# A linear-attention and MLP block on one core: v is never formed, column sums go to GpSimd, and nearly all projections become 64-row matmuls

## The chip, the cores and the metric

The kernel runs on one core of a Trainium2 chip. A core has a matrix engine (TensorE, "PE" in the profile; its weight loads are shown apart as "PEld"), VectorE ("DVE"), ScalarE ("ACT"), GpSimd ("POOL") and a queue engine that starts DMAs ("SP"). In this kernel PE accumulates into eight PSUM banks, and VectorE and ScalarE empty them. The metric is device microseconds for one execution. The profile counts from the first to the last instruction and is about 1.7 us shorter than that time.

The granted clock of TensorE differs from run to run (0.96 to 1.00 as a mean), so it is given with the times.

## The reference

```python
xn = layernorm(x)                              # x: 2048 tokens x 448, bf16
q, k, v = split(xn @ wqkv)                     # 16 heads of 28
pq, pk = phi(q), phi(k)                        # phi(t) = t+1 if t>0 else exp(t), + 1e-6
kv = einsum("bhsd,bhse->bhde", pk, v)          # summed over all tokens
z  = einsum("bhsd->bhd", pk)
o  = (pq @ kv) / (pq . z + 1e-6)
s  = o @ wo
g  = silu(relu(xn @ w1 + b1)**2 @ w2 + b2)     # 1792 hidden units
return x + s * g
```

As v is linear in xn, sum over tokens of pk^T v = (sum over tokens of pk^T xn) Wv. That is the identity that the change uses.

## The kernel before

The kernel keeps all on the chip. It lists operations, and a small scheduler of its own gives each engine a fixed order and assigns the PSUM banks when the program is built; at run time each engine follows its list and waits on semaphores. The 2048 tokens are 16 tiles of 128, or 4 groups of 512. The feature dimension, 448, is three chunks of 128 rows and one of 64. The transposed input `xT` holds this last chunk twice, on partitions 0 to 63 and 64 to 127, so that the 64-row remainders of two accumulators run on the two halves of the array at once (in the trace the two matmuls of such a pair start 3 to 4 ns apart):

```python
def pe_two(a, b, n, mm, reads, first):            # two accumulators
    lo, hi, full = slice(0, 64), slice(64, 128), slice(0, 128)
    if first:
        mm(e, 0, lo, 3, True, False)              # the 64-row pair
        mm(e, 1, hi, 3, True, False)
        for w in (0, 1):
            for c in range(3):                    # six 128-row matmuls
                mm(e, w, full, c, False, c == 2)
    else:
        ...                                       # six 128-row ones, then the pair

def kv(si):                                       # k and v of a token tile
    pe_two(kb, vb, D, ...)
    phi(kb, pk[:, si, :], ...)                    # ACT exp, DVE min+add, DVE max
    add("act", ... activation(out=va[:, si, :, 0:PD], in_=ps(vb)..., func=AF.Copy))

def kvt(g):                                       # pk^T v of four token tiles
    for si in range(4 * g, 4 * g + 4):
        for c in range(4):
            e.matmul(ps(kvb)[0:KA, c*PD:(c+1)*PD], va[:, si, c, 0:KA], pk[:, si, c*PD:(c+1)*PD], ...)
```

`va` has columns of ones beside v, so z comes out of the same matmuls. After the four groups, `kv` is folded with `wo`, the denominators are formed, and a last stage multiplies by w2 and writes the output.

## Time and profile before

| kernel before | value |
|---|---|
| time, first comparison | 165.28 us median of 4 runs (165.13 to 166.94) |
| span in the profile | 163.6 us |
| projections, sums and folds | 9.6 to 103.2 us |
| last stage (w2, output) | 103.2 to 163.6 us |

The page's first part (busy us, share of the span, instructions), and its fourth (the chain of waits: shares of the span by engine, then by line):

```profile
PE 153.2 (94%) x919; PEld 74.6 (46%) x927; DVE 102.2 (62%) x240; ACT 75.2 (46%) x135; POOL 20.2 (12%) x37
...
PE 89%; DMA 4%; DVE 2%; SPq 2%; issue 1%; DVEq 0%
```

PE is busy nearly always, and the chain stays on PE. To find out what PE loses while "busy", starts have to be read, as matmuls overlap. The timeline of PE around 68 us (start, duration, engine, line, operation, shape of the weights, output):

```profile
67.50 0.38 PE L595 MATMUL pb<-xT,w 128*128 128x512 bf16 x1
67.81 0.39 PE L595 MATMUL pb<-xT,w 64*128 64x512 bf16 x2
68.04 0.38 PE L595 MATMUL pb<-xT,w 64*128 64x512 bf16 x2
68.35 0.39 PE L595 MATMUL pb<-xT,w 128*128 128x512 bf16 x1
68.58 0.38 PE L595 MATMUL pb<-xT,w 128*128 128x512 bf16 x1
```

Each row after the first starts 0.31, 0.23, 0.31 and 0.23 us after the one before it. In undisturbed stretches 512-column matmuls start every 0.216 us. A step from 128 rows to 64 or back, called a mode step below, costs about 0.095 us; a pair (x2) costs no more than one matmul. The time from one start to the next is called a slot.

### The profile page before, as it was taken

What the parts mean: (1) busy time and instruction counts of PE and PEld (TensorE: products, weight loads), DVE (VectorE), ACT (ScalarE), POOL (GpSimd) and SP (SyncE); (2) the same over time, 40 slices, a digit from 0 to 9 for tenths busy, and PEclk for the clock granted to TensorE, in tenths of its full rate; (3) what the DMA queues carried; (4) which work ended last, traced back from release to release, by engine and by line L of the source; (5) the groups of instructions that cost most, each with busy time, mean ns of one, the idle gap of its engine ahead of it and who ended that gap; (6) DMA issues with size and microseconds to landing.
All of it is one profiled execution on the core that took longest, in us unless ns stands there. A gap on an engine that the chain in (4) does not pass through costs nothing.

```text
span 163.6 us, 2398 instructions
## 1 busy us (share of the span) xinstructions
PE 153.2 (94%) x919; PEld 74.6 (46%) x927; DVE 102.2 (62%) x240; ACT 75.2 (46%) x135; POOL 20.2 (12%) x37
## 2 busy tenths in 40 slices
PE   6568899999999999999999999999999999999990
PEld 6434445444435543454544444444455555555550
DVE  0688998688894756755584757399943433443373
ACT  3133677676675675766666756821121111121110
POOL 8600000000000000000000000000004432224352
PEclk9999999999999999999999999999999999999997
DMA  4999960000000000000000000000000011100013
GB/s 144 326 402 331 379 179 0 0 4 2 0 0 0 4 0 0 0 0 4 0 0 0 0 6 0 0 0 0 4 0 28 28 56 40 48 28 28 28 39 129
DMA packets 7158, 9.15 MB, mean 56 GB/s; under 512 B 556, under 2 KB 6252, under 8 KB 7148
## 3 DMA queue, kind: packets, MB, share of 16 engines
q1 hardware_dynamic: 6588, 8.09, 15.2%
q10 hardware_dynamic: 560, 0.92, 1.6%
q8 instruction: 7, 0.11, 0.3%
q14 instruction: 3, 0.02, 0.0%
HBM read 7.17 MB, written 1.84 MB: 55 GB/s over the span
## 4 chain that ended last, share of the span: by engine, by line
PE 89%; DMA 4%; DVE 2%; SPq 2%; issue 1%; DVEq 0%
PE pb L595 28%; PE pb L716 26%; PE pb L561 13%; PE pb L581 8%; PE pb L744 7%; DMA x_tok<-in_A_x_dram 4%; PE pb L626 2%; PE pb L466 2%; SPq L378 2%; PE pb L695 1%; DVE xT L478 1%; PE pb L668 1%; PE pb L649 1%; DVE st L413 0%; DVE obuf L753 0%
## 5 line engine op out<-in xcount | busy, mean ns | idle before, releaser
L595 PE MATMUL pb<-xT,w 128*128 128x512 bf16 (+1 forms) x216 | 46.8, 381 | 0.6 <-issue 0.3
L716 PE MATMUL pb<-w,r 128*128 128x448 bf16 x224 | 44.9, 353 | 0.0
L606 ACT ACTIVATE r<-pb,b1f 128x512 bf16<-128x512 f32 x56 | 35.2, 687 | 17.9 <-PE pb L595 17.9
L758 POOL TENSOR_TENSOR obuf<-obuf,x_tok 128x448 bf16<-128x448 bf16 x14 | 14.3, 1031 | 139.1 <-DVE obuf L753 139.1
L716 PEld LDWEIGHTS pb<-w,r 128*128 128x128 bf16 x224 | 21.5, 98 | 20.9 <-issue 1.3
L614 DVE TENSOR_TENSOR r<-r 128x512 bf16<-128x512 bf16 x56 | 22.4, 420 | 11.9 <-ACT r L606 11.8
L595 PEld LDWEIGHTS pb<-xT,w 128*128 128x128 bf16 (+1 forms) x224 | 17.2, 97 | 26.4 <-issue 10.9
L733 ACT ACTIVATE gbuf<-gbuf 128x448 bf16<-128x448 bf16 x16 | 9.2, 577 | 42.0 <-DVE gbuf L725 42.0
L725 DVE TENSOR_TENSOR gbuf<-pb,b2b 128x448 bf16<-128x448 f32 x16 | 10.0, 625 | 25.1 <-PE pb L716 24.7
L561 PE MATMUL pb<-w_qkv,xT 128*128 128x448 bf16 (+1 forms) x128 | 24.1, 354 | 1.7 <-DVE xT L478 1.6
L561 PEld LDWEIGHTS pb<-w_qkv,xT 128*128 128x128 bf16 (+1 forms) x128 | 9.8, 97 | 14.9 <-issue 5.6
L581 PE MATMUL pb<-xT,w_qkv 128*112 128x512 bf16 (+1 forms) x64 | 14.3, 387 | 0.0
L744 PE MATMUL pb<-msb,pqT 112*128 112x448 bf16 x64 | 13.9, 352 | 0.0
L538 ACT ACTIVATE pk<-pb 128x448 bf16<-128x448 f32 x16 | 8.7, 546 | 10.0 <-PE pb L561 10.0
L413 DVE BATCH_NORM_STATS2 st<-x_tok 128x6 f32<-128x448 bf16 x16 | 9.3, 614 | 5.9 <-DMA x_tok<-in_A_x_dram 5.9
L753 DVE TENSOR_TENSOR obuf<-pb,gbuf 128x448 bf16<-128x448 f32 x16 | 10.0, 625 | 2.1
L550 DVE SCALAR_TENSOR_TENSOR pqT<-pb,pqT 112x512 bf16<-112x512 f32 x16 | 10.7, 686 | 0.2
L538 ACT ACTIVATE pqT<-pb 112x512 bf16<-112x512 f32 x16 | 8.8, 596 | 4.4 <-PE pb L581 4.3
L550 DVE SCALAR_TENSOR_TENSOR pk<-pb,pk 128x448 bf16<-128x448 f32 x16 | 9.9, 619 | 0.2
L703 DVE TENSOR_TENSOR pqT<-pqT,pb 112x512 bf16<-112x512 bf16 x16 | 9.9, 679 | 0.0
L581 PEld LDWEIGHTS pb<-xT,w_qkv 128*112 128x112 bf16 (+1 forms) x64 | 6.9, 129 | 6.5 <-issue 3.1
L744 PEld LDWEIGHTS pb<-msb,pqT 112*128 112x128 bf16 x64 | 6.2, 97 | 5.9
(51 smaller groups left out, 81.9 us busy)
## 6 DMA issues: line engine op xcount, KB each, us to landing
out_dram<-obuf SPq DMA_DIRECT2D x16, 112.0 KB, 1.7
w<-in_B_w_dram SPq DMA_DIRECT2D x1, 1568.0 KB, 14.6
x_tok<-in_A_x_dram SPq DMA_DIRECT2D x3, 448.0 KB, 10.0
w<-in_B_w_dram SPq DMA_DIRECT2D x1, 1344.0 KB, 9.0
w_qkv<-in_A_wqkv_dram ACTq DMA_DIRECT2D x1, 672.0 KB, 5.0
x_tok<-in_A_x_dram SPq DMA_DIRECT2D x2, 224.0 KB, 4.4
w<-in_B_w_dram SPq DMA_DIRECT2D x2, 224.0 KB, 9.5
w_o<-in_A_wo_dram SPq DMA_DIRECT2D x1, 392.0 KB, 15.5
```

Of the source, the lines that this page charges most:

```text
L538: "act", lambda e, _: e.activation(out=slot, in_=ps(buf)[0:rows, 0:n], func=AF.Exp), [buf, "actw"],
L550: lambda e, _: e.scalar_tensor_tensor(out=slot, in0=ps(buf)[0:rows, 0:n], scalar=1.0 + 1e-6, in1=slot, op0=ALU.add, op1=ALU.max),
L561: return e.matmul(ps((kb, vb)[w])[:, 0:D], xT[rows, c, si * P : (si + 1) * P], w_qkv[rows, c, col : col + D], start=start, stop=stop,)
L581: return e.matmul(ps(bufs[w])[0:PD, 0:512], w_qkv[rows, c, col : col + PD], xT[rows, c, g * 512 : (g + 1) * 512], start=start, stop=stop,)
L595: return e.matmul(ps(bufs[w])[:, 0:512], w_1[rows, c, col : col + P], xT[rows, c, g * 512 : (g + 1) * 512], start=start, stop=stop,)
L606: lambda e, _, fi=fi, slot=slot, buf=bufs[w]: e.activation(out=slot, in_=ps(buf)[:, 0:512], func=AF.Relu, bias=b1f[:, fi : fi + 1]),
L614: return e.tensor_tensor(out=slot, in0=slot, in1=slot, op=ALU.mult)
L716: last = e.matmul(ps(b)[:, 0:D], r2[:, fi, si * P : (si + 1) * P], w_2[:, fi, :], start=(fi == 0), stop=(fi == NF - 1),)
L725: "dve", lambda e, _: e.tensor_tensor(out=gs, in0=ps(b)[:, 0:D], in1=b2b[:, :], op=ALU.add),
L744: last = e.matmul(ps(b)[:, 0:D], pqT[0:PD, c, si * P : (si + 1) * P], msb[0:PD, c, 0:D], start=(c == 0), stop=(c == 3),)
L753: "dve", lambda e, _: e.tensor_tensor(out=ob, in0=ps(b)[:, 0:D], in1=gs, op=ALU.mult),
L758: return e.tensor_tensor(out=ob, in0=ob, in1=x_tok[:, si, :], op=ALU.add)
```

## The change

Its intent: take PE's work down (no v, no separate k-by-v sums), take most of the mode steps out (64-row matmuls only, but for the first four k tiles, which keep the old form), and take four of ScalarE's evictions per group away. The core of the diff, with cuts:

```diff
-def kv(si): ...                        # k and v
-def kvt(g): ...                        # pk^T v, with the ones for z
+def pe_four(a, b, c, d):               # four accumulators, 64-row matmuls only
+    # lower half: a and b in four steps each, then c and d in three; upper half: c, d, then a, b
+    for lo, hi, us in ((0, 4, (a, c)), (4, 8, (b, d)), (8, 11, (c, a)), (11, 14, (d, b))):
+        for i in range(lo, hi):
+            for h in (0, 1):
+                u, k, start, stop = steps[h][i]
+                u[2](e, half[h], k, start, stop)
+def zsum(i):                           # z: running sum of pk, on GpSimd
+    add("pool", ... e.tensor_tensor(out=o[:, :], in0=pk[:, 0, :] if i == 1 else zacc[:, :],
+                                    in1=pk[:, i, :], op=ALU.add), ...)
+def token_sum(c):                      # xn^T pk over all 16 tiles, chunk c
+    for si in range(NT):
+        if c < 3:
+            e.matmul(ps(b)[:, 0:D], xn[:, si, c*P:(c+1)*P], pk[:, si, :], ...)
+        else:                          # 64 columns: even and odd tiles side by side
+            r = slice(64 * (si % 2), 64 * (si % 2) + 64)
+            e.matmul(ps(b)[r, 0:D], xn[:, si, 384:448], pk[:, si, :], ...)
+def fold_wv(): ...                     # times Wv, head by head; z from 4 one-column matmuls
@@ the order of PE
+quads(g, "Q0 H0 Q1 H1 Q2 H2 Q3 H3 ...")      # K, Q, H: k, q, h accumulators
+token_sum(0) ... token_sum(3); quads(g, "H6 H8 H7 H9"); fold_wv(); quads(g, "H10 H12 H11 H13")
@@ the start
+ln(0, 1); ln(1, 2); ln(2, 4)           # smaller layernorm steps; tiles 1 and 3 on ScalarE
+load_k("act", w_qkv, A_wqkv, "wk", D, 2 * D)  # Wk alone first, Wv last
```

The scheduler's rule also changes: a slightly later operation may be taken first if it is more urgent. The squares of h, which nothing needs until the last stage, are so put off.

## The prediction

> **What bounds it now.** TensorE. The page's first part has PE busy 94% of 163.6 us; the chain of waits puts 89% of the span on PE. In the timeline the first K/V matmul starts at 9.6 us; projections (q, k, v, h), k-by-v sums and folds run to 103.2 us; the last stage (w2, output) is untouched. Start to start, a 512-column matmul takes 0.216 us, a 448-column one 0.189 us, and two 64-row matmuls on the two halves of the array start 3 to 4 ns apart, so a pair costs one slot.
>
> **Where PE loses time.** Every step between a 128-row and a 64-row matmul adds 0.095 us to the spacing (0.312 instead of 0.216). Between 9.5 and 103.2 us some 66 such steps cost 6.5 us. This agrees with the Trainium skill, "TensorEngine Tiling (Array Packing)", Key Properties: changing the tiling mode drains the engine. Some 2.1 us more are three stalls at the start, PE waiting for VectorE's copy of xT. Hardly anything else is idle there.
>
> **What the change does to PE (estimates from those spacings).**
> - q, k, h in 64-row pairs: four accumulators still need 14 slots, so streaming is unchanged, but of the mode steps only some 14 remain (transposes, token sums, folds), 1.3 us: saves 5.2 us. The 250 additional pairs cost 3 to 7 ns each: 1.3 us back.
> - v goes: 56 slots, 10.6 us; the old k-by-v sums too, 64 x 0.053 = 3.5 us. Added: token sums, 56 slots, 10.6 us, and the fold with Wv, 1.0 us. Saves 2.5 us.
> - Start: separate layernorms, half the first weights, no v, so q/h begins sooner; but K0 now waits for two transposed tiles, and VectorE still queues the statistics of tiles 2 and 3 ahead of the first normalisation. Saves 1 to 3 us.
>
> **What moves elsewhere.** ScalarE loses 16 evictions of 0.54 us. VectorE has the same work in a shorter stage: some 14 us of phi, layernorm and xT per group plus 6 us of squares, against 17 us of PE. It fits because the squares are ordered late, into the token sums. ScalarE needs 4 x 0.69 = 2.75 us per quad of h against 3.02 us of PE: tight; I allow 1.5 us of PE waits. GpSimd takes 15 adds of about 1.1 us, off the path; by the Trainium skill, "GPSIMD Engine Reference", section 1, it shares SBUF interfaces with VectorE, so some VectorE operations may stretch; no trace here shows that yet.
>
> **Sum.** 5.2 - 1.3 + 2.5 + 2 + 0.3 (short folds) - 1.5, about 7.5 us, nearly all on the critical path: 165.4 to 157.6 us. Range 154.5 to 161.5.
>
> **What would show it.** First w2 matmul at about 95 us instead of 103.2; 64-row pairs spaced 0.216 to 0.223 us; under 20 mode steps; PE idle under 3 us between first K and first w2 matmul; token sums in 10.6 us; the last stage as long as before.
>
> **What would make it wrong.** Pairs that overlap worse in long runs (twice the weight loads): 0.01 us per slot costs 3 us. PE waiting by several us for evictions. VectorE stretched by GpSimd. w1 landing late, as h starts earlier (before, it landed at about 14 to 16 us).
>
> Chances: faster by over 2%: 0.92; within 2%: 0.07; slower: 0.01.

## More of the kernel before

VectorE's groups, by shape (count, then busy us and mean ns of one; then idle time before them):

```profile
L614 DVE TENSOR_TENSOR r<-r 128x512 bf16<-128x512 bf16 x56 | 22.4, 420 | 11.9 <-ACT r L606 11.8
L550 DVE SCALAR_TENSOR_TENSOR pk<-pb,pk 128x448 bf16<-128x448 f32 x16 | 9.9, 619 | 0.2
L432 DVE TENSOR_SCALAR xn<-x_tok,mv,rstd 128x448 bf16<-128x448 bf16 x16 | 5.5, 390 | 0.6 <-ACT rstd L425 0.6
L543 DVE TENSOR_SCALAR pk<-pk 128x448 bf16<-128x448 bf16 x16 | 4.4, 273 | 3.3 <-ACT pk L538 3.2
L446 DVE COPY xn<-xn 128x256 bf16<-128x256 bf16 x3 | 0.7, 220 | 0.0
```

These means are what the same operations are to be held against later: squares 420 ns, normalisation (`xn<-x_tok`) 390 ns, min-and-add of phi (`pk<-pk`) 273 ns, doubling of the last chunk (`xn<-xn`) 220 ns.

## The result

In the first comparison the changed kernel took 159.14 us (median of 4 runs, 159.10 to 159.31), the one before 165.28 us. The ratio, taken as the mean time of one kernel's fast runs over that of the other's of the same rounds and so not quite the ratio of the medians, is 0.961 (95% interval 0.955 to 0.967). The result is 1.5 us above the predicted 157.6 us, within the stated range. The first w2 matmul came at about 97 us, not 95.

The same parts of the page for the changed kernel:

```profile
PE 148.4 (94%) x1131; PEld 76.5 (49%) x1131; DVE 105.9 (67%) x237; ACT 70.8 (45%) x129; POOL 35.4 (22%) x49
...
PE 86%; DVE 6%; DMA 3%; SPq 2%; ACT 1%; issue 0%; DVEq 0%
```

PE's busy time falls by 4.8 us. VectorE's rises by 3.7 us, though it has almost the same operations, and 6% of the chain lie on VectorE, where it was 2%. Between the projections' matmuls the mode steps are gone, as the timeline of PE around 22 us shows: the rows start 0.21 to 0.22 us apart, and each window holds two pairs (x4), so a pair takes the time of one matmul, with nothing added:

```profile
22.20 0.59 PE L597 MATMUL pb<-xT,w 64*128 64x512 bf16 x4
22.42 0.59 PE L597 MATMUL pb<-xT,w 64*128 64x512 bf16 x4
22.63 0.59 PE L597 MATMUL pb<-xT,w 64*128 64x512 bf16 x4
22.85 0.59 PE L597 MATMUL pb<-xT,w 64*128 64x512 bf16 x4
```

Two things were not expected. First, the chain of waits between 46 and 58 us leaves PE for 8 us:

```profile
48.23 0.99 ACT pk L542 x2
49.52 1.06 DVE pk L554 x2
50.59 1.33 DVE xn L421 x2
51.91 1.21 DVE pk L547 x2
53.13 1.06 DVE pk L554 x2
54.19 1.34 DVE xn L421 x2
55.55 1.03 DVE xn L449
56.63 1.07 PE pb L463 x16
```

The transposes of the fourth group (L463) wait for the doubling of the last chunk (L449), that waits for the normalisations (L421), and these are longer than before. PE idles; the list of waits (who, for whom: us in total, times, longest) has it as its longest wait within the projections:

```profile
PE pb L463 <- DVE xn L449: 2.2, 2, 1.9
```

VectorE's groups show which operations grew:

```profile
L612 DVE TENSOR_TENSOR r<-r 128x512 bf16<-128x512 bf16 x56 | 20.6, 433 | 7.5 <-ACT r L606 7.5
L554 DVE SCALAR_TENSOR_TENSOR pk<-pb,pk 128x448 bf16<-128x448 f32 x16 | 9.6, 619 | 0.3
L421 DVE TENSOR_SCALAR xn<-x_tok,mv,rstd 128x448 bf16<-128x448 bf16 x14 | 6.2, 492 | 0.1
L547 DVE TENSOR_SCALAR pk<-pk 128x448 bf16<-128x448 bf16 x16 | 6.8, 432 | 4.6 <-ACT pk L542 4.6
L449 DVE COPY xn<-xn 128x256 bf16<-128x256 bf16 x3 | 1.5, 489 | 0.1
```

The one that reads PSUM (L554) still takes 619 ns. The other three, which read and write SBUF alone, grew: 273 to 432 ns, 390 to 492, 220 to 489. The timelines of VectorE and GpSimd, laid beside each other, say when:

```profile
50.50 1.41 DVE L421 TENSOR_SCALAR xn<-x_tok,mv,rstd 128x448 bf16<-128x448 bf16 x2
...
50.66 2.33 POOL L575 TENSOR_TENSOR zacc<-zacc,pk 128x448 f32<-128x448 f32 x2 [12.98 <-DVE pk L554]
54.34 2.15 POOL L575 TENSOR_TENSOR zacc<-zacc,pk 128x448 f32<-128x448 f32 x2 [1.34 <-DVE pk L554]
...
55.55 1.02 DVE L449 COPY xn<-xn 128x256 bf16<-128x256 bf16 x1
```

The second normalisation of the first row starts at 50.81 us, inside the first GpSimd add, and ends at 51.91, just after that add (51.78). The copy at 55.55 us starts just after the add of 55.46 us and ends just after it (56.57 and 56.49 us). Counted over the whole trace, operations that meet an add exceed the median of their own kind by 7.5 us in all, half a microsecond per add; bn_stats (the layernorm statistics, which read and write SBUF too: 611 ns alone, 617 with an add) and the PSUM-sourced phi step (618 and 624) don't grow. This agrees with the Trainium skill, "GPSIMD Engine Reference", section 1 (Specifications): GpSimd's SBUF interfaces are shared with VectorE, and instructions of VectorE in a two-port mode or with two SBUF inputs contend. The trace doesn't tell which mode an instruction ran in.

Second, after its idle time PE ran slow. The columns of this view of 57.70 to 61.00 us are the busy time and count of each engine, then the granted clock, the DMA share and GB/s. First the run of the first comparison, then a later run of the same kernel:

```profile
57.70:61.00 3.30, 3.30 (x18) 1.47 (x20) 2.08 (x5) 0.61 (x1) 0.00 (x0) 0.53 0.00 0
```

```profile
57.70:61.00 3.30, 3.30 (x32) 1.71 (x34) 2.19 (x6) 1.36 (x3) 0.00 (x0) 1.00 0.00 0
```

At a granted clock of 0.53, PE started 18 matmuls in this stretch, at 1.00 it started 32. Pairs were 0.42 us apart instead of 0.216 in the slow stretch, and the excess sums to 1.6 us. The later run has the same wait, but no slow stretch, and took 157.6 us.

The two traces suggest why. In their clock records the changes lie 3.413 us, or a multiple of it, apart, but for the last of each: in the first run at 6.73, 57.93 and 61.34 us; in the later one at 4.52 us and not again before 154.71. Counted on from 6.73 and 4.52 us in steps of 3.413, the wait of the first run lies whole in the step from 54.51 to 57.93 us, at the end of which the clock fell; that of the later run is cut in two at 55.72 us. PE's busy time (second column) in these steps, the first run and then the later one:

```profile
54.51:57.93 3.42, 1.48 (x22) 1.11 (x22) 3.39 (x6) 2.46 (x5) 1.90 (x2) 1.00 0.00 0
52.31:55.72 3.41, 2.36 (x22) 0.97 (x18) 3.38 (x6) 2.52 (x6) 1.99 (x3) 1.00 0.00 0
55.72:59.13 3.41, 2.52 (x30) 1.72 (x32) 3.41 (x8) 1.61 (x3) 0.75 (x1) 1.00 0.00 0
```

So whether the same wait costs a slow stretch would depend on where it falls on this grid. No run was made to test it.

The last stage was left alone and shows it (the columns are as above; the first row is the last stage before the change, then the changed kernel's projections and last stage):

```profile
103.20:163.60 60.40, 56.50 (x308) 28.16 (x304) 30.50 (x51) 11.83 (x19) 14.31 (x14) 0.98 0.10 31
9.10:97.35 88.25, 85.53 (x765) 42.44 (x766) 69.59 (x169) 55.68 (x102) 15.84 (x15) 0.98 0.19 57
97.35:157.60 60.25, 56.38 (x304) 28.11 (x302) 31.98 (x55) 11.98 (x20) 14.32 (x14) 0.99 0.10 31
```

### The profile page after: what moved, and what is told of

It is laid out like the page before. It is cut to its first block, busy times and chain, and to the rows that moved or that the text cites. A ratio compares the mean times of both kernels' runs of the same rounds, so it can differ in the third digit from the quotient of the medians.

```text
span 157.6 us, 2827 instructions
## 1 busy us (share of the span) xinstructions
PE 148.4 (94%) x1131; PEld 76.5 (49%) x1131; DVE 105.9 (67%) x237; ACT 70.8 (45%) x129; POOL 35.4 (22%) x49
## 4 chain that ended last, share of the span: by engine, by line
PE 86%; DVE 6%; DMA 3%; SPq 2%; ACT 1%; issue 0%; DVEq 0%
PE pb L755 27%; PE pb L597 25%; PE pb L783 8%; PE pb L585 7%; PE pb L564 6%; PE pb L626 6%; DMA b1r<-in_B_b_dram 3%; PE pb L463 3%; DVE xn L421 2%; SPq L365 2%; DVE pk L554 1%; PE pb L632 1%; DVE pk L547 1%; PE pb L734 1%; DVE xT L473 1%; DVE xn L449 1%
## 5 line engine op out<-in xcount | busy, mean ns | idle before, releaser
L597 PE MATMUL pb<-xT,w 64*128 64x512 bf16 x392 | 48.2, 381 | 0.0
L597 PEld LDWEIGHTS pb<-xT,w 64*128 64x128 bf16 x392 | 19.0, 95 | 22.6 <-issue 1.4
L612 DVE TENSOR_TENSOR r<-r 128x512 bf16<-128x512 bf16 x56 | 20.6, 433 | 7.5 <-ACT r L606 7.5
L575 POOL TENSOR_TENSOR zacc<-zacc,pk 128x448 f32<-128x448 f32 x13 | 13.7, 1055 | 46.8 <-DVE pk L554 45.4
L585 PE MATMUL pb<-xT,w_qkv 64*112 64x512 bf16 x112 | 15.7, 395 | 0.0
L564 PE MATMUL pb<-w_qkv,xT 64*128 64x448 bf16 (+1 forms) x100 | 12.8, 350 | 1.3 <-DVE xT L473 0.8
L554 DVE SCALAR_TENSOR_TENSOR pqT<-pb,pqT 112x512 bf16<-112x512 f32 x16 | 10.9, 688 | 0.3
L585 PEld LDWEIGHTS pb<-xT,w_qkv 64*112 64x112 bf16 x112 | 7.5, 133 | 5.9 <-issue 1.3
L542 ACT ACTIVATE pk<-pb 128x448 bf16<-128x448 f32 x16 | 7.8, 540 | 5.1 <-PE pb L564 5.1
L547 DVE TENSOR_SCALAR pk<-pk 128x448 bf16<-128x448 bf16 x16 | 6.8, 432 | 4.6 <-ACT pk L542 4.6
L554 DVE SCALAR_TENSOR_TENSOR pk<-pb,pk 128x448 bf16<-128x448 f32 x16 | 9.6, 619 | 0.3
```

Source lines behind the costliest of these rows:

```text
L542: "act", lambda e, _: e.activation(out=slot, in_=ps(buf)[0:rows, 0:n], func=AF.Exp), [buf, "actw"],
L554: lambda e, _: e.scalar_tensor_tensor(out=slot, in0=ps(buf)[0:rows, 0:n], scalar=1.0 + 1e-6, in1=slot, op0=ALU.add, op1=ALU.max),
L564: return e.matmul(ps(b)[:, 0:D], xT[rows, c, si * P : (si + 1) * P], w_qkv[rows, c, D : 2 * D], start=start, stop=stop)
L575: lambda e, _: e.tensor_tensor(out=o[:, :], in0=pk[:, 0, :] if i == 1 else zacc[:, :], in1=pk[:, i, :], op=ALU.add),
L585: return e.matmul(ps(b)[0:PD, 0:512], w_qkv[rows, c, m * PD : (m + 1) * PD], xT[rows, c, g * 512 : (g + 1) * 512], start=start, stop=stop,)
L597: return e.matmul(ps(b)[:, 0:512], w_1[rows, c, fi * P : (fi + 1) * P], xT[rows, c, g * 512 : (g + 1) * 512], start=start, stop=stop,)
```

## The experiments

Two theories stood for the wait at 54 us. Theory A: the GpSimd adds hold up VectorE's SBUF-to-SBUF operations; where these lie ahead of the transposes, PE waits, and then pays again with the clock. Theory B: VectorE simply has too much to do, or in a bad order, in a stage that became shorter. A third question was what the 64-row form itself is worth. Twelve runs of four executions each were made, in three jobs, each job on one chip together with the kernel before, whose medians there were 167.8, 166.4 and 166.8 us (slow runs included). The changed kernel itself ran in the second job only; the first job, on another chip, has e3 in its place, which is the same program but for 36 added matmuls.

### e1: the adds almost taken away

```diff
-o = zb if i == NT - 1 else zacc
-... out=o[:, :], in0=... zacc[:, :], in1=pk[:, i, :]
+o, w = zb if i == NT - 1 else zacc, slice(0, D if i in (1, NT - 1) else 1)
+... out=o[:, w], in0=... zacc[:, w], in1=pk[:, i, w]
```

> 13 of the 15 GpSimd adds handle one column instead of 448 (z is wrong on purpose); every engine's order is the same as in the changed kernel. Theory A (the adds hold up VectorE's SBUF-to-SBUF operations, so the transposes of group 3 wait, so PE idles 2.1 us and then runs 1.6 us longer at half clock): VectorE's tensor_scalar on pk and xn return from means of 432 and 492 ns to about 275 and 390 ns, the copy of the tails from 1023 to 220 ns, the PE wait at 54 us and the dip of the granted clock vanish, 155.4 us (154.9 to 156.2). Theory B (VectorE's work is just too much or too late for the shortened stage): the wait stays above 1 us and the time above 157.5 us.

The time was 155.49 us (155.24 to 155.62). The result is wrong, as meant. The order of every engine is the same. PE's wait at 54 us and the slow clock are gone, and VectorE's groups are as they were before the change:

```profile
L421 DVE TENSOR_SCALAR xn<-x_tok,mv,rstd 128x448 bf16<-128x448 bf16 x14 | 4.8, 391 | 0.1
L547 DVE TENSOR_SCALAR pk<-pk 128x448 bf16<-128x448 bf16 x16 | 4.4, 280 | 5.8 <-ACT pk L542 5.8
L449 DVE COPY xn<-xn 128x256 bf16<-128x256 bf16 x3 | 0.7, 223 | 0.1
```

That is theory A's number, and 2.3 us under e3 of the same job, which has the wait but in three of four runs no slow clock. B falls as the only cause: the same order and the same VectorE work cause no wait once the adds don't run beside it.

### e2: the normalisation moved out of the way, the adds left

ScalarE's `rstd` of the last four tiles was ready for computing at 45 us but stood in ScalarE's list at 50.2 us. A bonus in the scheduler moves it ahead; the list of PE and GpSimd stays the same.

```diff
 add("act", ... activation(out=rstd[:, c], in_=vep[:, c], func=AF.Exp, scale=-0.5), ...)
+.boost = 20.0 if lo == 12 else 0.0        # subtracted from the operation's latest start
```

> Correct kernel. ScalarE computes the rstd of tiles 12 to 15 right after the logarithm, 5 us earlier than in the changed kernel; VectorE can then normalise these tiles at about 45 us, before the GpSimd adds of the group start at 50.7 us. Adds, PE order and all else as in the changed kernel. Theory A as refined (contention costs only where a blocked operation lies on PE's path): the sum of VectorE's stretch stays at 5 us or more, but the PE wait at 54 us and the clock dip vanish: 155.4 us (154.9 to 156.3). Rival (any stretch of VectorE is paid for in time): 158 us or more.

The time was 155.98 us (155.81 to 156.35), and the result is correct. VectorE normalised the four tiles in one row, before the first add of that group at 50.32 us:

```profile
44.91 1.31 DVE L422 TENSOR_SCALAR xn<-x_tok,mv,rstd 128x448 bf16<-128x448 bf16 x4 [0.65 <-ACT rstd L414]
```

The wait of the transposes vanished. A small new one (0.4 us by the list of waits) stood at 56 us: an accumulator of q waited for a min-and-add that an add had stretched to 1.12 us. So order was a second ingredient: with a better order the same contention is almost free here. The 2.1 us took both, adds running beside the normalisations and normalisations standing late in the list; taking away either one removed them.

### e3: PE kept busy through the wait

```diff
+if g == 2:
+    warm(36, dur=0.01)                    # 36 matmuls on the identity, result unused
 pe_transpose([4 * g + 4, 4 * g + 5])
```

> Correct kernel. 36 matmuls on the identity (about 2.0 us) are put in front of the group-3 transposes, where PE waits; all other orders are the same. If the half-speed stretch after the wait is the clock gate answering PE's idleness, it vanishes while the wait of the transposes stays (they start at 56.6 us as before): about 157.5 us (157.2 to 158.0), and PEclk shows no dip. Rival (the dip has another cause, say power or the run of 64-row matmuls): dip stays, 159.1 us.

The median was 157.79 us; the runs were 157.40, 157.75 and 157.84 us at a granted clock of 1.00, and 159.13 us at 0.985, which is the run that was profiled. In this profile the stretch after the wait ran at full clock:

```profile
57.70:61.00 3.30, 3.30 (x45) 2.38 (x44) 3.30 (x9) 1.16 (x2) 0.30 (x1) 1.00 0.00 0
```

and the slow stretch it does have lies elsewhere, at 9.2 to 12.6 us, right at the start. This agrees with a dip that answers PE's idleness and can be prevented without shortening the wait, but it does not prove it. On the 3.413 us grid of this trace a border (56.99 us) cuts the wait (56.13 to 58.15 us) in two, so that perhaps no dip would have come without the added matmuls either; and of the four runs of the unedited kernel in after_again, below, two kept their clock too. The Trainium skill, "TensorE: Matmul & The Clock Gate", Part 1, tells of such a gate, which falls to half clock after an idle window of about 3.4 us; the window is free-running. The 3.413 us grid of the traces agrees with such a window, but it need not be wholly idle: in the trace of the first comparison about 2 us of idle time within one such stretch sufficed. Only two of the eight runs of the changed kernel have a trace, one with the dip and one without; six of the eight have the time and mean clock of one dip, but where the untraced ones had it is not known (e3's run of 159.13 us had it at the start).

### e5 and its repetition: z on PE

```diff
-zsum(i) on GpSimd, 15 adds
+for si in range(NT):                      # four column strips of 32 at once
+    r = slice(32 * (si % 4), 32 * (si % 4) + 32)
+    e.matmul(ps(b)[r, 0:D], ones[:, :], pk[:, si, :], start=(si < 4), stop=(si >= NT - 4))
+... one ScalarE eviction; the fold multiplies by 1/32 instead of 1
```

> Correct kernel. The column sums move from GpSimd to PE: 16 matmuls with a 32-column stationary of ones, on four column strips at once, and one ScalarE eviction. VectorE is free of GpSimd in the projections; PE gets about 4 slots of 0.19 us and two mode steps, 0.95 us. Theory A: 155.4 + 0.95 = 156.3 us (155.8 to 157.0), no wait at 54 us. Theory B: no gain, 159.5 to 160 us.

156.47 us (156.25 to 156.61), correct. It costs PE about 1 us more than e1, as estimated from the slots, and there is no stretch on VectorE. The repetition in the third job:

> The kernel of run e5 (column sums on PE), unedited, so that the next one stands beside it on one chip: 156.5 us again (156.2 to 156.7).

Its median was 156.60 us, from 156.01, 156.43 and 156.77 us, and one run of 158.10 us at a granted clock of 0.989. That run has no trace; this kernel has no wait at 54 us, so some clock can be lost without it.

### after_again: the changed kernel once more

> The changed kernel itself, unedited, so that it stands beside the kernel before and the next three on one chip. The first comparison gave 159.1 against 165.3 us; on the chip of the last four runs the kernel before took 166.7 to 168.9 us. If that chip or day is slower for both, the changed kernel is slower by the same 1.5%; if only the kernel before varies (its granted clock was 0.964 to 0.99 in those runs), the changed kernel stays near 159.1 us.

The four runs were 157.60 and 157.89 us at a granted clock of 0.996 and 0.998, and 159.13 and 159.50 us at 0.985 and 0.986: the same program, with a mean clock as with and without one slow stretch. Neither alternative of the expectation is quite right; both kernels vary. The kernel before took 165.0 to 165.3 us at 0.995 to 1.00, 166.4 to 166.5 us at 0.984 to 0.985, and, in its slow run, 167.7 us at 0.979 in this job. At full clock the comparison is thus about 165.1 against 157.7 us. Where the kernel before loses its clock in those runs was not seen: the runs without a profile have no trace.

### e4 and e10: q, k and h multiplied as before

```diff
-pe_four(*us)
+pe_two(us[0], us[2], False)
+pe_two(us[1], us[3], True)
```

> Correct kernel. The changed kernel with q, k and h multiplied as before: per two accumulators six 128-row matmuls and one 64-row pair (42 groups); v still not formed, the sums still on GpSimd. By the prediction the 64-row form is worth some 42 mode steps of 0.095 us, 4.0 us, minus what the additional pairs cost (0 to 1.7 us), so this run takes 162 to 163.5 us if nothing else moves. If the pairs saved less than thought: 160 us or less. The wait at 54 us may shift, as the scheduler sees another timing; its size is to be read off and taken out.

158.95 us (158.71 to 159.09), far under the 162 expected. The trace shows why: in this kernel's list the last normalisations stand at 44 to 46 us, ahead of the adds, and PE doesn't wait at 54 us nor lose its clock. Undoing the 64-row form had undone the wait too, so the comparison was blurred. e10 does it again in the kernel that has no adds:

> Run e5 with q, k and h as in run e4 (six 128-row matmuls and one 64-row pair per two accumulators). No GpSimd adds and so, in either form, no wait in the projections: the difference from e5_again is the worth of the 64-row form alone. Counting mode steps in the traces of e4 (some 44, 4.2 us) and e1 (14, 1.3 us) gives 2.9 us: 159.4 us (159.0 to 160.0). If the 64-row form were worth only what e4 against the changed kernel suggests (0 to 0.4 us), this is under 157.2 us; if as much as predicted (5.2 less 1.3 us), 160.4 us.

159.77 us (159.70 to 160.06) against 156.60 us (156.01 to 158.10) for e5_again of the same rounds, 3.2 us by the medians. That is the worth of the 64-row form alone where nothing else interferes; counted from start to start, the mode steps of e10 (50, 4.7 us) cost 3.0 us more than those of e5_again (18, 1.7 us).

### e11: the same lists, the adds later

```diff
-zsum(1..3) after group 0, zsum(4..7), zsum(8..11) after their groups
+all of zsum(1..11) only when xT of tile 15 is there; zsum(12..15) as before
```

> Correct kernel. The order of work on every engine is exactly that of the changed kernel and all 15 adds stay on GpSimd; they only may not start before xT of tile 15 is there (about 55 us), past the last normalisation. Theory A (time lost because adds and normalisations coincide): no wait at 54 us, no clock dip, 155.4 to 156.2 us, though VectorE's total stretch stays above 4 us (now mostly on the squares). Theory B: no change, 157.6 us without and 159.1 us with the dip.

163.56 us (162.78 to 164.02): 4.4 us above the first comparison's 159.14 us, where a gain of 3 us was expected. The first half of the expectation held: the transposes ran at 55.0 us without a wait. But eleven adds then ran back to back, and VectorE's list had ten squares in a row at that point (VectorE, then GpSimd):

```profile
61.38 10.32 DVE L612 TENSOR_TENSOR r<-r 128x512 bf16<-128x512 bf16 x10
...
59.55 11.53 POOL L575 TENSOR_TENSOR zacc<-zacc,pk 128x448 f32<-128x448 f32 x10
```

Ten squares that take 0.34 us from start to start elsewhere took 1.03 us each on average, and most of them 1.17 us from start to start, in step with the adds. Behind them stood the phi of a k tile, an accumulator stayed full, PE waited 4.8 us and then lost its clock again: on this trace's grid the step from 68.18 to 71.59 us has no PE work at all, and half clock followed it for 6.8 us. The expectation was wrong in taking the squares for harmless because nothing waits for them: VectorE follows its list in order, and here the phi that PE needed stood behind them.

### e7, e8 and e9: looking for the best version

```diff
+e7: e2, and at the start: tile 0 normalised before the statistics of tile 3,
+    b1 transposed after the first k tiles, "Q0 Q2 Q1 Q3" before the first h
+e8: e5 and the same start
+e9: e11's late adds, the early rstd, and the same start
```

> Correct kernel, meant to beat all so far: the early rstd of the run e2 (156.0 us), and at the start the normalisation of tile 0 ahead of the statistics of tile 3, the b1 transposition after the first K tiles, and four q accumulators before the first h ones. PE stalls of 0.34, 0.68 and 0.95 us stand before and between the first K matmuls; I expect 0.5 to 1.2 us less: 154.8 to 155.5 us. If the arrival of x or w1 sets the start instead, no change: 156.0 us.

156.68 us (156.66 to 156.70): no gain over e2. The start was better, but a wait for q's phi at 56 us grew from 0.4 to 1.3 us (by the list of waits), again behind squares and min-and-adds held up by adds:

```profile
PE pb L598 <- DVE pqT L555: 1.3, 1, 1.3
```

> Correct kernel. As e7, but with the column sums on PE (run e5, 156.5 us) in place of the early rstd: 0.5 to 1.2 us less than e5, 155.3 to 156.0 us; slower than e7 by about 0.4 us if the early rstd really frees PE's path, faster than e7 if VectorE's stretch of 7 us still costs somewhere.

156.09 us (156.08 to 156.10), correct, 0.4 us under e5. The second alternative of its expectation held: faster than e7, since VectorE's stretch still cost there.

> Correct kernel, meant as the best: e11 with the start of e8 (0.4 us less than e5 at the start): 155.0 to 155.8 us. If the delayed adds end after the fold with Wv needs them, or hold up q's evictions in the last group, PE waits show at 70 to 92 us and the gain is lost.

155.58 us (155.55 to 155.60), correct, the best of all: 0.938 of the kernel before in the same rounds (0.930 to 0.947). The adds still cost VectorE 6.1 us, but between 13 us and the last stage no PE start is more than 0.16 us late, mode steps included. This list, too, has ten squares in a row beside the adds. Here, unlike in e11, the squares ran at full speed and one add was held up instead, for 4.40 us (VectorE, then GpSimd):

```profile
61.07 3.42 DVE L613 TENSOR_TENSOR r<-r 128x512 bf16<-128x512 bf16 x10
60.99 4.40 POOL L576 TENSOR_TENSOR zacc<-zacc,pk 128x448 f32<-128x448 f32 x1
```

So either engine can hold up the other; what decides it was not tested. e8 is 0.5 us slower but does not depend on that outcome, and has no GpSimd work beside VectorE's in the projections.

## Why the prediction was right

The total was right: 157.6 us was foretold, 159.1 us came, and 157.6 to 157.9 us in the runs in which the clock stayed up. That it met the number so closely at full clock is in part luck: the waits were worse than foretold and the pairs better, and the two cancel in part. The table adds up PE's starts from the first K matmul to the first w2 matmul in the trace of the kernel before and in that of after_again, which had full clock; positive is time saved.

| term | predicted | measured |
|---|---|---|
| mode steps (66 to 14 foretold, 68 to 17 counted) | 5.2 us | 4.9 us |
| pairs dearer than single matmuls; slots after a step | -1.3 us | 0.9 us |
| v and k-by-v sums out (10.5 + 3.2), token sums and fold in (10.6 + 0.8) | 2.5 us | 2.3 us |
| start: first K, stalls in group 0, one transposition | 2 us (1 to 3) | 1.8 us |
| short folds | 0.3 us | 0.1 us |
| PE waits in the projections | -1.5 us | -2.1 us |
| sum | 7.2 us (called about 7.5) | 7.9 us; the first w2 matmul comes 7.7 us sooner |
| half clock after the wait (traced once; time and clock of 6 of 8 runs fit one such stretch) | not foreseen | -1.6 us |

- Mode steps: read off rightly, and so was the mechanism. The Trainium skill, "TensorEngine Tiling (Array Packing)", Key Properties, says that a change of mode drains the engine; the trace puts it at 0.095 us. The worth of the 64-row form of q, k and h alone is 3.2 us (e10); the rest went with v's groups and the old sums.
- The fear that pairs overlap worse in long runs was unfounded: they start 0.216 us apart, as single matmuls do. Besides, most of the slots that were 0.01 us longer after a step (0.044 us in q) are gone too.
- Token sums, fold and start came out as costed. In the profile of the first comparison the 48 full token-sum matmuls took 9.2 us and the 16 half ones 1.6 us; q began at 13.6 us instead of 18.3, of which 2.65 us are v's 14 slots.
- The last stage kept its length, as foretold (60.4 and 60.25 us).
- The failed step is "I allow 1.5 us of PE waits", with ScalarE's evictions of h as the reason. No such wait exists in the trace. The wait came from normalisations held up by the GpSimd adds, which the prediction called off the path, with only the remark that "some VectorE operations may stretch". They stretched by 7.5 us in all, of which 2.1 us reached PE (e1: without them no wait). The loss of clock, 1.6 us more in the traced run of the first comparison, was not foreseen at all. So this term cost 3.7 us there in place of 1.5; the better pairs made up for most of that.

## What to carry to other kernels

If accumulations mix full-height and half-height matmuls, count the mode steps from start to start: putting everything in half-height pairs cost nothing per pair here and removed 0.095 us per step. An engine that is "off the path" can still lengthen the path: before placing elementwise work on GpSimd, look which SBUF-to-SBUF operations of VectorE will run beside it (here tensor_scalar, copy and tensor_tensor stretched, bn_stats did not) and what stands behind them in VectorE's list. A PE wait of some two microseconds may be paid nearly twice, as in the first comparison; whether unused matmuls in the gap prevent that is not shown here (e3).

## What the Trainium skill lacked or had wrong

- "GPSIMD Engine Reference", section 1, names the contention but gives no durations; only these, not the fact that one engine holds up the other, are lacking in the skill. A GpSimd add of 1.03 to 1.13 us held a 0.27 us tensor_scalar of VectorE to as much as 1.05 us, a 0.22 us copy to 1.02 us and a 0.42 us tensor_tensor to 1.26 us; the blocked operation ended 0.08 to 0.15 us after the add (once 0.28). Fifteen adds cost VectorE 7.5 us. Ten squares beside a row of adds took 1.17 us from start to start in e11; in e9 they took 0.34 us, and one add 4.40 us.
- "TensorEngine Tiling (Array Packing)", Key Properties, has the drain but no duration: 0.095 us per change between 128-row and 64-row matmuls, in either direction, and about 0.01 us in the slot after it (0.044 us in q).
- "TensorE: Matmul & The Clock Gate", Part 1, has the half clock come after an idle window of about 3.4 us: here a stretch of 3.42 us in which PE was still busy for 1.48 us brought 3.41 us at half clock, while stretches with 2.36 and 2.52 us of 3.41 busy (after_again) brought none.
